# Two weight loads with a cast on the way, replaced by one load each and casts on ScalarE and GpSimd

## The chip, the cores and the metric

The kernel runs on one core of a Trainium2 chip. The metric is the device time of one launch in microseconds (us), the median over several runs. A core has five engines that run side by side and wait for each other through semaphores: TensorE (PE, matmuls, with its weight loads shown as PEld), VectorE (DVE), ScalarE (ACT), GpSimd (POOL) and SyncE (SP). Transfers between the device's memory and the core's on-chip memory are issued from a queue of SP or POOL and carried out by 16 DMA engines.

## What is computed

An attention with a few inducing points, followed by a feed-forward layer with a hard-swish. `x` is 4 batches of 12480 rows of 128 columns, `inducing` is 32 rows, the feed-forward layer is 2048 wide.

```python
def mab(q, kv):
    s = scale * (q @ kv.transpose(0, 2, 1))
    s = s - s.max(-1, keepdims=True)
    a = np.exp(s)
    a /= a.sum(-1, keepdims=True) + 1e-09
    return a @ kv
h = mab(I, x)                      # 32 x 128 for each batch
x2 = mab(x, h)                     # 12480 x 128 for each batch
u = x2 @ w_in                      # 128 -> 2048
g = u * np.clip(u + 3.0, 0.0, 6.0) / 6.0
out = g @ w_out                    # 2048 -> 128
```

## The kernel before

The kernel does not run the wide layer row by row. As long as the pre-activations stay small, hard-swish is a polynomial of second degree, and each row of the attention's output is a mixture of 32 rows of `h`; so the output of a row is a linear term plus a quadratic form in its 32 weights, and the coefficients of both can be made once for each batch. A check at the end (`bad_i`) leads to a direct path if that does not hold.

Each batch goes through three stages:

- **a**, the first attention: rows of x are cast to bf16 (`xb`), transposed on PE (`pt`, copied to `xT`), multiplied with the inducing points (`s`), exponentiated on ACT (`a`), and summed into `hnd` on PE; DVE sums the weights into `dacc`, the denominators.
- **c**, the coefficients: the column sums of the denominators on PE (`dps`, with a matrix of ones), their reciprocal (`rD`, DVE), the transposed `hnd` (`H` on ACT, `htp` on PE), their product `HT` (DVE), and from it `HTr` (ACT), `dH`, `W`, `Wd` (DVE). PE then multiplies `w_in_r` with `HTr` (`gp`, the linear part) and `w_in_b` with `dH` (`dpm`, the quadratic part); ACT and DVE square `dpm` into `sq`; PE multiplies `sq` with `w_out_b` (`cp`) and the activated `gp` with `w_out_r` (`lp`). The results are `BD` and `Cq`.
- **b**, the output: 25 chunks a batch, each with exponentials `TF` on ACT, products `TD` of them with a spread-out factor `d` on DVE, and matmuls `op` on PE with `BD` (line 795) and `Cq` (line 811), scaled into `os` by DVE and stored by SP. The factor `d` is spread over partitions by a DMA of SP (line 758), four chunks ahead.

The order on every engine is the order in which the program issues its instructions (`manual_schedule`); there is no planner. For batch 0, stage a runs alone (`a_first`), then stage c (`c_first`), then a loop of 100 chunks: chunk t of stage b with pieces of stages a and c of the next batch laid between by `fill`.

Loads of x are issued from POOL's queue, in this order before the loop: the seven loads of batch 0 (some in two parts), the four weight loads of `load_weights` (lines 158 to 163), the first two of batch 1. `w_in_b` and `w_out_b` are bf16 in on-chip memory, so their loads cast on the way; `w_in_r` and `w_out_r` keep 32 bits. The other four loads of batch 1 are held back: `load_held` (line 132) issues them when POOL has read a column of the fourth spread `d`, through the small copy `seen`. POOL is in order, so what stands before `seen` on POOL also stands before these loads. `xr` has five buffers; a load waits until its buffer has been read.

In `a_first`, the denominators end up in three pieces: `dacc` (folded by four adds on POOL, line 419), `dlast` (reduced on DVE, line 413 through 444) and the last piece (line 406 through 444). `c_den_part` adds one matmul with ones for each piece; a 32-bit matmul shows up as two passes on PE. `warm(n)` (line 174) issues n matmuls of zeros, 128x512, whose result nothing reads.

`c_first` opens like this:

```python
warm(1)
c_den(0)      # H on ACT, dps on PE, rD on DVE
warm(1)
c_HT(0)       # htp on PE, HT on DVE, HTr and HTb on ACT, dH W Wd on DVE
warm(1)
c_G(0, 0, 6)  # gp on PE
```

Of the kernel before, what the change touches and what calls it, by code (L numbers as in the profile page):

```python
# [9 lines left out]
FP32 = mybir.dt.float32  # L10
# [30 lines left out]
def kernel(  # L41
# [8 lines left out]
    nc = tc.nc  # L50
# [3 lines left out]
    F = moe_w_in.shape[1]  # L54
    FB = F // P
# [25 lines left out]
    with ExitStack() as es:  # L81
# [71 lines left out]
        w_in_b = const.tile([P, F], BF16, name="w_in_b")  # L153
        w_in_r = const.tile([P, F], FP32R, name="w_in_r")
        w_out_b = const.tile([P, FB, C], BF16, name="w_out_b")
        w_out_r = const.tile([P, FB, C], FP32R, name="w_out_r")

        def load_weights():
            w_out = moe_w_out.rearrange("(kb kp) c -> kp kb c", kp=P)
            nc.gpsimd.dma_start(w_in_b[:, :], moe_w_in[:, :])  # L160
            nc.gpsimd.dma_start(w_in_r[:, :], moe_w_in[:, :])
            nc.gpsimd.dma_start(w_out_b[:, :, :], w_out)
            nc.gpsimd.dma_start(w_out_r[:, :, :], w_out)


# [8 lines left out]
        def warm(n):  # L174

            wp = psF.tile([P, 512], FP32, name="wp", tag="fb")
            for _ in range(n):
                nc.tensor.matmul(wp[:, :], lhsT=wake[:, :P], rhs=wake[:, :])
# [57 lines left out]
        def side_bank(b, shape, dtype, name):  # L236

            if b == 0:
                turn[0] += 1
                if turn[0] % 2:  # L240
                    return psO.tile(shape, dtype, name=name, tag="op")
            return psF.tile(shape, dtype, name=name, tag="fb")
# [99 lines left out]
        def a_first():  # L342

            st = S[0]
            pieces = [(g, h, h + 8) for g in range(XBUF + 1) for h in (0, 8)]
            pieces.insert(2, (NF, 0, SL))
            last = len(pieces) - 1
            a1s = {}

            def cast(k):  # L350
                g, lo, hi = pieces[k]
                p = groups[g][1]
                if lo == 0:
                    xbs[(0, g)] = xbin.tile([P, TG, C], BF16, name="xb")
                xb, xf = xbs[(0, g)], xs[(0, g)]
                if hi - lo == 8 and (lo == 0 or k == last):
                    cuts = [(nc.scalar.copy, lo, lo + 4), (nc.vector.tensor_copy, lo + 4, hi)]
                else:
                    cuts = [(nc.scalar.copy, lo, hi)]
                for eng, i, j in cuts:  # L360
                    eng(xb[:p, i:j, :], xf[:p, i:j, :].bitcast(FP32))

            def transpose(k):
                g, lo, hi = pieces[k]
                t0, p, n = groups[g]
                step = 4 if k == last else 8
                for i in range(lo, hi, step):
                    j = min(i + step, hi)
                    pt = side_bank(0, [P, 1024], BF16, "pt")
                    for q in range(i, j):  # L370
                        nc.tensor.transpose(pt[:, (q - i) * p : (q - i + 1) * p], xbs[(0, g)][:p, q, :], ident_b[:p, :p])
                    eng = nc.scalar.copy if k == last and i > lo else nc.vector.tensor_copy
                    eng(st["xT"][:, t0 + i * p : t0 + j * p], pt[:, : (j - i) * p])

            def weights(k):
                g, lo, hi = pieces[k]
                t0, p, n = groups[g]
                s1 = side_bank(0, [P, 512], FP32, "s1")
                for q in range(lo, hi):
                    nc.tensor.matmul(  # L380
                        s1[:p, (q - lo) * M : (q - lo + 1) * M],
                        lhsT=st["xT"][:, t0 + q * p : t0 + (q + 1) * p],
                        rhs=I_T[:, :],
                    )
                w = (hi - lo) * M
                a1 = a1p.tile([P, TG * M], FP32R, name="a1")
                nc.scalar.activation(a1[:p, :w], s1[:p, :w], ACT.Exp, scale=scale)
                a1s[k] = a1

            def add(k):  # L390
                g, lo, hi = pieces[k]
                p, w, a1 = groups[g][1], (hi - lo) * M, a1s[k]
                for q in range(lo, hi):
                    nc.tensor.matmul(
                        st["hnd"][:M, :C],
                        lhsT=a1[:p, (q - lo) * M : (q - lo + 1) * M],
                        rhs=xs[(0, g)][:p, q, :],
                        start=(k == 0 and q == lo),
                        stop=(k == last and q == hi - 1),
                    )  # L400
                f = a1[:p, :w].bitcast(FP32)
                d = st["dacc"][:p, lo * M : hi * M]
                if g == 0:
                    nc.vector.tensor_copy(d, f)
                elif k == last:
                    c_red(0, f, p, hi - lo)
                elif k == last - 3:
                    st["dlast"] = cst.tile([P, 8 * M], FP32, name="dlast")
                    nc.vector.tensor_copy(st["dlast"][:, :], f)
                elif k > last - 3:  # L410
                    nc.vector.tensor_add(st["dlast"][:, :], st["dlast"][:, :], f)
                    if k == last - 1:
                        c_red(0, st["dlast"][:, :], P, 8)
                else:
                    nc.vector.tensor_add(d, d, f)
                if k == last - 4:
                    d = st["dacc"]
                    for h in (8, 4, 2, 1):
                        nc.gpsimd.tensor_add(d[:, : h * M], d[:, : h * M], d[:, h * M : 2 * h * M])
                    st.setdefault("dred", []).append(d[:, :M])  # L420
                if hi == groups[g][2]:
                    load_next(0, g)

            for k in range(3):
                cast(k)
            transpose(0)
            for k in range(last + 1):
                if k < last:
                    transpose(k + 1)
                weights(k)  # L430
                if k + 3 <= last:
                    cast(k + 3)
                if k:
                    add(k - 1)
                if k == 3:
                    half_rows()
            add(last)


        def c_red(b, src, p, n):  # L440
            st = S[b]
            st["reds"] = st.get("reds", -1) + 1
            dred = cst.tile([P, M], FP32, name=f"dred{st['reds']}")
            nc.vector.tensor_reduce(
                dred[:p, :], src.rearrange("p (s m) -> p m s", m=M), axis=AX.X, op=ALU.add
            )
            st.setdefault("dred", []).append(dred[:p, :])
# [182 lines left out]

        def c_first():

            warm(1)
            c_den(0)
            warm(1)
            c_HT(0)
            warm(1)
            c_G(0, 0, 6)
            sq = lambda *jbs: [c_sq(0, jb) for jb in jbs]
            cs = lambda *jcs: [c_C(0, jc) for jc in jcs]  # L640

            sg = lambda jb: (c_sq(0, jb), c_G(0, jb + 6, jb + 7))
            sg(0)
            sg(1)
            sg(2)
            b_pack(0, 0)
            b_e(0, 0)
            for c in range(4):
                b_spread(0, c)
            a_cast(1, 0, ((nc.gpsimd.tensor_copy, 0, 2), (nc.gpsimd.tensor_copy, 2, 4)))  # L650
            load_held(3)
            for jb in range(3, 7):
                sg(jb)
                cs(jb - 3)
            sg(7)
            b_f(0, 0)
            cs(4)
            sg(8)
            b_base(0, 0, 0)
            cs(5)  # L660
            sg(9)
            c_hs(0)
            b_base(0, 0, 1)
            cs(6)
            sq(10)
            cs(7)
            sq(11)
            b_r(0, 0)
            cs(8)
            sq(12)  # L670
            cs(9)
            sq(13)
            cs(10)
            b_base(0, 1, 0)
            sq(14)
            cs(11)
            sq(15)
            cs(12)
            c_L(0, 0)
            c_L(0, 1)  # L680
            b_base(0, 1, 1)
            c_BD(0)
            cs(13, 14, 15)
            b_prod(0, 0)
            c_tail(0)
            b_pack(0, 1)
            b_e(0, 1)
            c_max(0)
# [400 lines left out]
```

## Time and profile before

| what | us |
|---|---|
| median of 6 runs | 313.83 |
| lowest and highest | 313.18, 315.82 |
| the profiled execution | 313.89 |
| its span, first to last instruction | 312.1 |
| PE busy in the span | 298.3 |
| first matmul of `c_first` (a warm) | 24.87 |
| first `op` of the loop (line 795) | 39.74 |
| the same of batch 1 and of batch 2 | 114.46, 187.77 |
| granted TensorE clock, mean | 0.994 of full |

Times inside the profile count from the span's start. A line of the order of time has the start, the length, the engine, the line of the code, the operation, what it writes and reads, its shape and how many; in brackets the time that the engine was idle before it and what ended that. A line of the DMA issues ends with the size in KB and the median time from issue to landing. A line of the chain has the start, the length and what it was. The loads issued from POOL are the rows "POOLq".

### The profile page before, as it was taken

Reading aid. Unit: us, or ns where it says so; the run is one execution under the profiler, and the core shown is the slowest. Engines: PE = TensorE matmul, PEld = TensorE weight load, DVE = VectorE, ACT = ScalarE, POOL = GpSimd, SP = SyncE. Lnnn points to the kernel's source line nnn. Section 1 sums busy time; section 2 is a strip of 40 time slices with the busy share of each in tenths; the row PEclk is TensorE's granted clock in tenths of the full one; section 3 lists DMA queues with packets and bytes.
Section 4 is the critical chain, followed back from the end, with each engine's and each line's share of the span. In section 5 each row is a group of like instructions: output and inputs, shape, how many; then the busy total and the mean of one; then the engine's idle time right before and its main releaser. Section 6 shows DMA issues by size and latency. Waiting matters only on the chain.

```text
span 312.1 us, 9579 instructions
## 1 busy us (share of the span) xinstructions
PE 298.3 (96%) x3930; PEld 233.4 (75%) x3930; DVE 236.1 (76%) x539; ACT 226.3 (73%) x417; POOL 27.1 (9%) x64
## 2 busy tenths in 40 slices
PE   6899999999999999999999999999999999999991
PEld 2797777887677878888767878888767786777780
DVE  2697895978884868888695768788787577888883
ACT  3785869886589678886679759888668936777750
POOL 7631230100100000001000000000000000000000
PEclk9999999999999999999999999999999999999997
DMA  7999879988963444899966525555245424666643
GB/s 218 414 340 285 312 237 396 308 312 264 335 229 130 109 165 83 276 321 318 321 201 188 177 97 137 205 155 185 86 137 189 159 50 170 202 215 213 221 168 155
DMA packets 26769, 67.73 MB, mean 217 GB/s; under 512 B 5184, under 2 KB 19552, under 8 KB 20832
## 3 DMA queue, kind: packets, MB, share of 16 engines
q1 hardware_dynamic: 18160, 38.36, 37.7%
q0 software_dynamic: 8560, 28.71, 29.9%
q8 instruction: 32, 0.52, 0.7%
q14 instruction: 17, 0.14, 0.1%
HBM read 29.77 MB, written 25.56 MB: 177 GB/s over the span
## 4 chain that ended last, share of the span: by engine, by line
PE 73%; DMA 10%; DVE 6%; ACT 4%; issue 2%; POOL 2%; SPq 0%; DVEq 0%; ACTq 0%; POOLq 0%
PE op L811 27%; PE bp L771 11%; PE op L795 7%; DMA xr<-in_x_dram 6%; PE hnd L292 6%; PE pt L270 4%; DMA d<-dk 4%; PE cp L592 4%; ACT sq L583 2%; PE s L278 2%; PE pp L742 2%; PE dpm L572 2%; PE ep L698 2%; PE sp L712 1%; DVE os L827 1%
## 5 line engine op out<-in xcount | busy, mean ns | idle before, releaser
L778 ACT ACTIVATE TF<-bp 128x512 bf16<-128x512 f32 (+1 forms) x200 | 116.7, 596 | 38.2 <-PE rp L731 21.0
L811 PE MATMUL op<-Cq,TF 128*128 128x128 bf16 (+1 forms) x800 | 109.3, 223 | 0.0
L811 PE MATMUL op<-Cq,TD 128*128 128x128 bf16 (+1 forms) x800 | 105.9, 219 | 0.0
L827 DVE TENSOR_TENSOR os<-op,r_all 128x512 f32<-128x512 f32 (+1 forms) x100 | 68.4, 684 | 18.6 <-PE op L811 17.8
L771 PE MATMUL bp<-xT,W 128*128 128x512 bf16 (+1 forms) x200 | 75.2, 376 | 0.6 <-ACT TF L778 0.5
L811 PEld LDWEIGHTS <-TF 128*128 128x128 bf16 (+1 forms) x800 | 50.5, 98 | 33.7 <-issue 24.7
L787 DVE TENSOR_TENSOR TD<-TF,d 128x1024 bf16<-128x1024 bf16 (+1 forms) x100 | 66.9, 669 | 5.2 <-ACT TF L778 3.4
L811 PEld LDWEIGHTS <-TD 128*128 128x128 bf16 (+1 forms) x800 | 61.3, 98 | 1.0 <-DVE TD L787 0.2
L795 PE MATMUL op<-BD,nf 128*128 128x512 f32 (+1 forms) x100 | 53.3, 533 | 0.5 <-DVE os L827 0.4
L583 ACT ACTIVATE sq<-dpm 128x512 bf16<-128x512 f32 x60 | 34.8, 629 | 5.5 <-PE dpm L572 3.1
L261 ACT CAST xb<-xr 128x1024 bf16<-128x1024 f32 x34 | 35.6, 1055 | 2.8 <-DMA xr<-in_x_dram 2.8
L732 DVE RECIPROCAL r_all<-rp 128x4 f32<-128x4 f32 (+1 forms) x100 | 17.8, 178 | 23.3 <-PE rp L731 22.9
L731 PE MATMUL rp<-one,nf 128*128 128x4 f32 (+1 forms) x100 | 34.5, 345 | 0.3
L271 DVE COPY xT<-pt 128x1024 bf16<-128x1024 bf16 (+1 forms) x42 | 25.8, 618 | 6.3 <-PE pt L270 5.8
L122 POOL DMA_DIRECT2D xr<-in_x_dram x25 | 13.6, 550 | 146.1 <-PE rp L731 44.9
L749 ACT ACTIVATE dk<-pp 128x512 bf16<-128x512 f32 (+1 forms) x28 | 15.7, 560 | 11.6 <-PE pp L742 10.2
L292 PE MATMUL hnd<-xr,a 128*32 128x128 f32 x288 | 24.1, 226 | 0.0
L572 PE MATMUL dpm<-dH,w_in_b 128*128 128x512 bf16 x64 | 23.3, 380 | 0.1
L270 PE MATMUL pt<-ident_b,xb 128*128 128x128 bf16 x300 | 23.3, 218 | 0.0
L771 PEld LDWEIGHTS <-W 128*128 128x128 bf16 x200 | 19.5, 97 | 5.0 <-issue 3.4
L592 PE MATMUL cp<-w_out_b,sq 128*128 128x128 bf16 x256 | 22.7, 220 | 0.0
L514 PE MATMUL gp<-HTr,w_in_r 128*128 128x32 f32 x64 | 21.3, 358 | 0.3 <-ACT HTr L492 0.3
(129 smaller groups left out, 391.4 us busy)
## 6 DMA issues: line engine op xcount, KB each, us to landing
out_dram<-os SPq DMA_DIRECT2D x24, 1024.0 KB, 4.1
xr<-in_x_dram POOLq DMA_DIRECT2D x21, 1024.0 KB, 7.5
d<-dk SPq DMA_DIRECT2D x96, 128.0 KB, 4.2
xr<-in_x_dram POOLq DMA_DIRECT2D x4, 512.0 KB, 8.2
x<-in_x_dram POOLq DMA_DIRECT2D x2, 512.0 KB, 13.9
w_in_r<-in_moe_w_in_dram POOLq DMA_DIRECT2D x1, 1024.0 KB, 15.7
w_out_r<-in_moe_w_out_dram POOLq DMA_DIRECT2D x1, 1024.0 KB, 17.5
w_in_b<-in_moe_w_in_dram POOLq DMA_DIRECT2D x1, 512.0 KB, 13.4
```

Source lines behind the costliest of these rows:

```text
L261: eng(xb[:p, lo:hi, :], xs[(b, g)][:p, lo:hi, :].bitcast(FP32))
L270: nc.tensor.transpose(pt[:, (i - lo) * p : (i - lo + 1) * p], xb[:p, i, :], ident_b[:p, :p])
L292: nc.tensor.matmul(st["hnd"][:M, :C], lhsT=a1[:p, i * M : (i + 1) * M], rhs=xs[(b, g)][:p, i, :], start=(g == 0 and i == 0), stop=(g == NG ...
L583: nc.scalar.activation(sq[:, :], dpm[:, :], ACT.Square)
L592: nc.tensor.matmul(st["cp"][:, k * C : (k + 1) * C], lhsT=sq[:, k * P : (k + 1) * P], rhs=w_out_b[:, jc, :], start=(jc == 0 and k == 0), s ...
L731: nc.tensor.matmul(rp[:p, :SL], lhsT=nf[:, j * p : (j + 1) * p], rhs=one4[:, :])
L771: nc.tensor.matmul(bp[:, :w], lhsT=st["W"][:, k].rearrange("p m i -> p (m i)"), rhs=st["xT"][:, c0 : c0 + w],)
L778: nc.scalar.activation(st[("x", c)][:, k, :w], bp[:, :w], ACT.Exp, scale=scale)
L787: nc.vector.tensor_mul(u[:, :, :w], t[:, :, :w], d[:, :w].unsqueeze(1).to_broadcast([P, 2, w]))
L795: nc.tensor.matmul(op[:p, :], lhsT=st[("nf", g)][:, j * p : (j + 1) * p], rhs=st["BD"][:, :], start=True, stop=False, skip_group_check=True,)
L811: nc.tensor.matmul(op[:p, s * C : (s + 1) * C], lhsT=T[k][:, s * p : (s + 1) * p], rhs=st["Cq"][:, k, :], start=False, stop=(s == SL - 1 a ...
L827: nc.vector.tensor_mul(ot[:p, j * SL : (j + 1) * SL, :], op[:p, :].rearrange("p (s c) -> p s c", c=C), r_all[:p, b, c, :].unsqueeze(2).to_ ...
```

## The change

It has four parts, all in the first batch.

1. `load_weights` loads only `w_in_r` and `w_out_r`; the two loads that cast to bf16 are gone.
2. `c_first` makes `w_in_b` from `w_in_r` with two copies on ACT, one ahead of `c_den(0)` (so ahead of `H`) and one behind it (ahead of `HTr`). It makes `w_out_b` from `w_out_r` with two copies on POOL, behind the folding adds and ahead of the casts of batch 1's first piece and of `seen`.
3. The folded `dacc` is added to the reduced `dlast` on DVE, between the two reduces, so that two pieces instead of three go into `dps`.
4. The first two `warm(1)` of `c_first` become `warm(2)`.

```diff
         def load_weights():
             w_out = moe_w_out.rearrange("(kb kp) c -> kp kb c", kp=P)
-            nc.gpsimd.dma_start(w_in_b[:, :], moe_w_in[:, :])
             nc.gpsimd.dma_start(w_in_r[:, :], moe_w_in[:, :])
-            nc.gpsimd.dma_start(w_out_b[:, :, :], w_out)
             nc.gpsimd.dma_start(w_out_r[:, :, :], w_out)
...
                     if k == last - 1:
                         c_red(0, st["dlast"][:, :], P, 8)
+                        d1, d2 = st["dred"]
+                        nc.vector.tensor_add(d2, d2, d1)
+                        st["dred"] = [d2]
...
         def c_first():
 
-            warm(1)
+            warm(2)
+            nc.scalar.copy(w_in_b[:, : F // 2], w_in_r[:, : F // 2].bitcast(FP32))
             c_den(0)
-            warm(1)
+            nc.scalar.copy(w_in_b[:, F // 2 :], w_in_r[:, F // 2 :].bitcast(FP32))
+            for h in (0, FB // 2):
+                hs = slice(h, h + FB // 2)
+                nc.gpsimd.tensor_copy(w_out_b[:, hs, :], w_out_r[:, hs, :].bitcast(FP32))
+            warm(2)
             c_HT(0)
             warm(1)
             c_G(0, 0, 6)
```

## The prediction

> **What bounds the kernel now.** I read the page first: busy shares, then the DMA issues, then the chain of waits, and only then the order of time from 5 to 60 us, because the diff touches nothing that runs later than 40 us except through what it makes late or early.
>
> ```profile
> span 312.1 us, 9579 instructions
> PE 298.3 (96%) x3930; PEld 233.4 (75%) x3930; DVE 236.1 (76%) x539; ACT 226.3 (73%) x417; POOL 27.1 (9%) x64
> ```
>
> TensorE (PE) is busy 96% of the span. From 40 us on it is the bound, so an edit is worth what it adds to or takes from PE's stalls, no more. Next, the DMA issues (KB each, us from issue to landing) and, from the order of time, the four weight issues on POOL:
>
> ```profile
> w_in_r<-in_moe_w_in_dram POOLq DMA_DIRECT2D x1, 1024.0 KB, 15.7
> w_out_r<-in_moe_w_out_dram POOLq DMA_DIRECT2D x1, 1024.0 KB, 17.5
> w_in_b<-in_moe_w_in_dram POOLq DMA_DIRECT2D x1, 512.0 KB, 13.4
> w_out_b<-in_moe_w_out_dram POOLq DMA_DIRECT2D x1, 512.0 KB, 16.5
> ```
> ```profile
> 10.26 0.55 POOL L160 DMA_DIRECT2D w_in_b<-in_moe_w_in_dram  x1
> 10.80 0.54 POOL L161 DMA_DIRECT2D w_in_r<-in_moe_w_in_dram  x1
> 12.79 1.17 POOL L162 DMA_DIRECT2D w_out_b<-in_moe_w_out_dram  x1 [1.45 <-DMA xr<-in_x_dram]
> 15.29 1.15 POOL L163 DMA_DIRECT2D w_out_r<-in_moe_w_out_dram  x1 [1.33 <-DVE xT L373]
> ```
>
> Issue plus time to landing gives when each arrives. The last piece of x for batch 0, by the view of tile x, was issued at 7.47 and took 13.9: 21.4. Then w_in_b 23.7, w_in_r 26.5, w_out_b 29.3, w_out_r 32.8. The view of tile xr has 19.1 as its longest, which is the load issued at 19.42: 38.5. The xr load issued at 16.85 lies between, by 35.7 (POOL starts its cast of it at 35.76). The steps are 2.3, 2.8, 2.8, 3.5, 2.9, 2.8 us: the queue works as a line, one load behind another, and a load that writes 512 KB costs nearly as much of it as one that writes 1024 KB.
>
> What hangs on that line is in the chain of waits (start, us, what), and then in the order of time:
>
> ```profile
> 31.93 7.56 DMA d<-dk
> 39.54 0.28 POOL seen L135
> 40.32 7.00 DMA xr<-in_x_dram
> ```
> ```profile
> 47.40 1.05 ACT L261 CAST xb<-xr 128x1024 bf16<-128x1024 f32 x1 [2.75 <-DMA xr<-in_x_dram]
> 49.00 0.38 PE L771 MATMUL bp<-xT,W 128*128 128x512 bf16 x1 [0.55 <-ACT TF L778]
> ```
>
> The fourth spread d waits 7.56 us behind the line; `seen` waits for d; the held loads of batch 1 wait for `seen`; the first big one takes 7.00 us and lands at 47.32; ACT has been idle for 2.75 us; TF, behind that cast on ACT, is late; PE stops. It is the one DMA wait of ACT in 40 to 60 us.
>
> **What the change removes.** Two loads, 2.3 + 2.8 = 5.1 us of the line. Nothing of x moves, since x stands ahead of the weights. w_in_r takes w_in_b's place: 21.4 + 2.8 = 24.2. w_out_r: 24.2 + 3.5 = 27.7. The two xr loads: 30.6 and 33.4. POOL also issues w_out_r and the two xr loads earlier (w_out_b waited 1.45 us for an xr load to land before it could go out, and the issues after it followed); a load still lands no earlier than its place in the line.
>
> Then d: the fourth spread is issued at 31.93 + 0.4 (the front's delay, below). It lands about 1 us after the line empties in the old run (39.5 against 38.5), which would be 34.4, but a spread on a quiet queue takes 2.5 us in the trace (the ones of 2.5 to 2.6 us near 117 to 122 us), so 34.8. `seen` follows, unless POOL is still casting: its last cast of batch 1's first piece ends at 30.6 + 2 x 1.04 = 32.7. The held load goes out at 40.32 - 4.7 = 35.6 and lands, at the same 7.0, at 42.6. ACT came to this cast at 47.40 - 2.75 = 44.65 and will at 45.0: the wait is gone with 2.4 us to spare, and the two loads behind it, 2.9 us each, arrive before their casts at 49.32 and 52.65 too.
>
> Worth on PE: from the op matmul at 48.17 to the bp at 49.00 passed 0.83, where the same pair at 45.61 and 45.73 took 0.12: 0.71. The pair of op at 49.44 and 49.73 took 0.29, at 43.23 and 43.35 0.12: 0.17. The 16 s matmuls at 49.85 took 0.84 (they wait for an xT copy that DVE had behind the late TD), those at 43.46 0.56: 0.28. Sum 1.16 us. Bounds: 0.55 (the wait the row itself names) and 1.41 (first op<-BD of a batch to the next batch's first: 39.74 to 114.46 is 74.72, 114.46 to 187.77 is 73.31). I take 1.16; after the stall ACT has to catch up, and without it nothing is late next that the trace shows.
>
> **What it adds ahead of the loop.** These are the rows between the last matmul of the first stage and the first of the second:
>
> ```profile
> 24.36 0.61 DVE L444 TENSOR_REDUCE dred<-dlast 128x32 f32<-128x256 f32 x1
> 24.89 0.58 DVE L444 TENSOR_REDUCE dred<-a 128x32 f32<-128x256 f32 x1
> 25.07 0.26 ACT L472 COPY H<-hnd 32x128 f32<-32x128 f32 x1 [0.75 <-PE hnd L394]
> 25.77 0.38 PE L178 MATMUL wp<-wake 128*128 128x512 bf16 x1
> 25.97 0.36 DVE L477 RECIPROCAL rD<-dps 128x32 f32<-128x32 f32 x1 [0.50 <-PE dps L460]
> 26.08 0.24 PE L483 MATMUL htp<-ident,H 32*128 32x32 f32 x1
> 26.44 0.23 DVE L486 TENSOR_TENSOR HT<-htp,rD 128x64 f32<-128x64 f32 x1
> 26.70 0.22 ACT L492 CAST HTr<-HT 128x32 fp32r<-128x32 f32 x1 [1.37 <-DVE HT L486]
> ```
>
> *The DVE add.* It needs the first reduce (ends 24.97) and POOL's last add (24.06 + 0.39 = 24.45, covered). No row shows a 128x32 add f32 alone; the nearest, L504 on 128x32 at 28.16, takes 0.20, with the next DVE instruction 0.10 behind it. So the second reduce starts at 24.97 + 0.04 + 0.10 = 25.11 instead of 24.89, +0.22, and with it dps and rD: 26.19.
>
> *Matmuls.* Six dps passes become four, which saves two steps of 0.11, but PE waits for the second reduce at that point: worth nothing. The first extra warm takes their place. The second, between dps and htp, is on the path: the warm at 24.87 holds PE until the first dps at 25.10, 0.23, and the chain puts 0.22 to a matmul of 512 columns. htp starts at 26.08 + 0.22 + 0.22 = 26.52, ends 26.76; HT at 26.84 instead of 26.44. Everything behind, HTr, gp, dH, dpm, moves by that: +0.40. Bounds: 0.22 (htp hidden behind rD) and 0.55 (eight warms in a row at 3.34 take 2.60 us, so (2.60 - 0.38) / 7 = 0.32 each, and 0.22 of the add).
>
> *ACT casts.* Each is 128x1024 f32 to bf16: 1.05 us by the L361 and L261 rows. The last Exp of the stage ends at 23.93 + 0.39 = 24.32 and w_in_r is there at 24.2. First half to 25.4, H (0.26) to 25.65, second half to 26.7, HTr wanted at 27.1. H is wanted by htp at 26.52. Both casts lie in ACT's idle time: 0. The cover is 0.4 us: if w_in_r lands after 24.6, the second half holds HTr, and each us of lateness is a us at the end.
>
> *POOL casts.* 1.04 each by the L261 POOL row. w_out_r at 27.7, halves done at 28.8 and 29.8; the first cp, which needs the first half, is at 29.56 + 0.40 = 29.96, the ninth some 4 us later. Behind them on POOL: the xr casts (wanted by PE at 40.9) and `seen`, both covered above. Cost 0, with a cover of 1.2 us.
>
> *POOL beside DVE.* These casts run while DVE makes dH and W from two SBUF operands. The rows for such a meeting: L411 adds, 0.42 us beside POOL's adds at 22.25 to 24.45, and L415 adds of the same shape 0.42 with POOL idle; but the L409 copy takes 0.44 beside POOL where the same copy at L404 takes 0.28 alone. So 0 to 2 x 1.04 = 2.08 if each cast shut DVE out entirely. I take 0, by the row of the same kind.
>
> [...]
>
> **Sum.** -1.16 + 0.40 = -0.76. The profiled execution took 313.89 (span 312.1 and 1.8 around it), 0.06 above the median 313.83 of the six. 313.89 - 0.76 = 313.13, less 0.06: 313.1.
>
> **Rivals.** *The stall is replaced* (0.15). PE waits as long for DVE or another tile in the first loop, and only the front's cost is left: 313.8 + 0.4 = 314.2. For it: DVE and ACT are at 2.00 of 2 us in several stretches there; against it: batch 1, with the same work, runs 1.41 shorter.
>
> *More is relieved* (0.17). All 1.41 comes back, the front is hidden, and PE's stop of about 0.5 us at 40.3 to 40.6 (op waiting for Cq) goes as well: 313.8 - 1.9 = 311.9. Against it: Cq waits for DVE work on cp, not for a load.
>
> *The line is not a line* (0.10), the slower one. If landings are paced by something other than the bytes ahead, w_in_r lands at 26.5 as now. ACT is in order, so H waits: 26.5 + 1.05 + 0.26 = 27.8, then htp, HT at 28.2, the second half until 28.9, HTr, gp at 29.1 instead of 26.96: +2.15, and no load is earlier, so nothing comes back: 313.8 + 2.15 = 316.0. Against it are six even steps of the line. Were the stall's gain kept, it would decide from a landing of 24.6 + 0.76 = 25.4 on.
>
> *POOL shuts DVE out* (0.08): 313.1 + 2.08 = 315.2.
>
> **How the numbers follow.** The forecast has 0.50, with 312.6 to 313.8 as its own range (stall 0.55 to 1.41, front 0.22 to 0.55). The range reaches down to the second rival and up to the last, 311.8 to 315.2, leaving out the third and tails. 0.5%, or 1.57 us, is about what a measurement of this kernel can tell from no change. Faster by more: the second rival, 0.17. Slower by more: the third and half of the last, 0.14. Within: 0.69.
>
> **What would show it.** Right: w_in_r lands near 24.2 and w_out_r near 27.7; HT starts 0.3 to 0.5 later; `seen` near 35; no DMA wait of ACT before the L261 cast near 45; a first batch within 0.5 us of 73.3. Wrong: an ACT cast of w_in ended by a DMA wait past 24.6; dH or W rows of 1 us or more; PE idle before cp; a stop of bp on TF that stays.

## The result, and the profile after

| | before | changed |
|---|---|---|
| median, us (runs) | 314.02 (71) | 317.44 (34) |
| ratio, changed to before | | 1.0077, 95% interval 1.0057 to 1.0098 |
| profiled execution, us | 313.89 | 318.12 |
| its span, us | 312.1 | 316.3 |
| mean granted TensorE clock in it | 0.994 | 0.986 |

The changed kernel is slower by 0.8%. The medians are of all runs; the ratio leaves out the slow ones, over 1.5% above the fastest of the same kernel, so it is not the quotient of the two medians. The forecast was 313.1 us and its range ended at 315.2.

The top of the page of the changed kernel shows where to look. In the line PEclk each digit is a fortieth of the span, 7.9 us, and 9 stands for 90% or more of full clock:

```profile
span 316.3 us, 9580 instructions
PE 302.0 (95%) x3930; PEld 235.2 (74%) x3930; DVE 239.0 (76%) x540; ACT 228.9 (72%) x419; POOL 27.8 (9%) x64
PEclk9999699999999999999999999999999999999998
L259 ACT CAST xb<-xr 128x1024 bf16<-128x1024 f32 x34 | 35.5, 1052 | 0.0
w_in_r<-in_moe_w_in_dram POOLq DMA_DIRECT2D x1, 1024.0 KB, 13.8
w_out_r<-in_moe_w_out_dram POOLq DMA_DIRECT2D x1, 1024.0 KB, 16.8
```

Three things stand there. The same 3930 matmuls kept PE busy for 302.0 us instead of 298.3, and the fifth slice, 31.6 to 39.5 us, has a reduced clock that the page of before has nowhere but in its last slice. The group of ACT casts on L259 has no idle time ahead of it; in the kernel before the same group (L261) had these 2.8 us:

```profile
L261 ACT CAST xb<-xr 128x1024 bf16<-128x1024 f32 x34 | 35.6, 1055 | 2.8 <-DMA xr<-in_x_dram 2.8
```

And the loads come early: issued at 10.28 and 10.82, w_in_r lands at 24.08 and w_out_r at 27.64; 24.2 and 27.7 had been worked out. So what was to be relieved was relieved. From the first `op` matmul of the loop to the first of batch 1 it is 45.29 to 118.86, 73.57 us, where the kernel before took 74.72 (how much of that the earlier loads are worth is taken up at e8). The loss lies ahead of that: the first `op` starts 5.55 us later than before, at 45.29 instead of 39.74.

In order of time (start, us, engine, line, operation), the front of the changed kernel:

```profile
27.00 0.22 DVE L487 TENSOR_TENSOR HT<-htp,rD 128x64 f32<-128x64 f32 x1 [0.25 <-PE htp L484]
27.25 0.58 DVE L499 TENSOR_TENSOR dH<-HT 128x256 bf16<-128x256 f32 x1
27.70 2.38 POOL L640 CAST w_out_b<-w_out_r 128x1024 bf16<-128x1024 f32 x2 [3.16 <-DMA w_out_r<-in_moe_w_out_dram]
27.75 1.42 DVE L500 TENSOR_TENSOR dH<-HT 128x256 bf16<-128x256 f32 x1
29.09 1.42 DVE L502 TENSOR_TENSOR W<-HT 128x256 bf16<-128x256 f32 x1
29.22 0.39 PE L573 MATMUL dpm<-dH,w_in_b 128*128 128x512 bf16 x1 [0.85 <-DVE dH L500]
30.27 2.13 POOL L259 CAST xb<-xr 128x1024 bf16<-128x1024 f32 x2 [0.19 <-ACT sq L584]
30.43 1.03 DVE L505 TENSOR_TENSOR Wd<-HT 128x32 bf16<-128x32 f32 x1
31.51 0.62 PE L748 MATMUL pp<-xT,Wd 128*32 128x512 bf16 x4 [1.37 <-DVE Wd L505]
33.37 0.63 PE L573 MATMUL dpm<-dH,w_in_b 128*128 128x512 bf16 x1
```

and the same DVE instructions of the kernel before, where POOL did nothing at that time:

```profile
26.70 0.58 DVE L498 TENSOR_TENSOR dH<-HT 128x256 bf16<-128x256 f32 x1
27.18 0.58 DVE L499 TENSOR_TENSOR dH<-HT 128x256 bf16<-128x256 f32 x1
27.68 0.58 DVE L501 TENSOR_TENSOR W<-HT 128x256 bf16<-128x256 f32 x1
28.16 0.20 DVE L504 TENSOR_TENSOR Wd<-HT 128x32 bf16<-128x32 f32 x1
```

The first `dH` takes 0.58 in both. From the moment POOL starts to cast, the other `dH` and `W` take 1.42 each and `Wd` 1.03 instead of 0.20. PE waits for them twice, 0.85 and 1.37 us, as the brackets say. And from then on the `dpm` matmul that took 0.39 at 29.22 takes 0.63 at 33.37: the clock. The view of stretches of the changed kernel gives it (stretch, length, busy us and instructions of PE, PEld, DVE, ACT, POOL, then granted clock, DMA share, GB/s):

```profile
28.00:30.77 2.77, 1.29 (x10) 0.89 (x9) 2.77 (x3) 1.11 (x2) 2.58 (x3) 1.00 0.91 349
30.77:37.60 6.83, 6.09 (x39) 4.21 (x40) 3.54 (x7) 3.37 (x6) 1.63 (x2) 0.50 0.37 87
```

PE was busy for 1.29 of the 2.77 us up to 30.77; then it had half its clock for 6.83 us.

Five distances in the order of time split the loss. They are used for every kernel below:

| us | before | changed | difference |
|---|---|---|---|
| start of `HT` | 26.44 | 27.00 | +0.56 |
| `HT` to first `dpm` | 1.48 | 2.23 | +0.75 |
| first `dpm` to first `pp` | 0.84 | 2.29 | +1.45 |
| first `pp` to first `op` | 10.99 | 13.77 | +2.78 |
| first `op` to batch 1's first `op` | 74.72 | 73.57 | -1.15 |

The rest of the span differs by -0.17; together that is +4.22. The two spans, 316.3 and 312.1, differ by 4.2.

### The profile page after: what moved, and what is told of

It is laid out like the page before. It is cut to its first block, busy times and chain, and to the rows that moved or that the text cites. A ratio compares the mean times of both kernels' runs of the same rounds, so it can differ in the third digit from the quotient of the medians.

```text
span 316.3 us, 9580 instructions
## 1 busy us (share of the span) xinstructions
PE 302.0 (95%) x3930; PEld 235.2 (74%) x3930; DVE 239.0 (76%) x540; ACT 228.9 (72%) x419; POOL 27.8 (9%) x64
## 4 chain that ended last, share of the span: by engine, by line
PE 78%; DVE 9%; DMA 7%; issue 2%; POOL 1%; ACT 1%; DVEq 0%; ACTq 0%; POOLq 0%
PE op L817 28%; PE bp L777 12%; PE op L801 7%; PE hnd L290 6%; PE cp L593 5%; PE pt L268 5%; DMA x<-in_x_dram 4%; PE dpm L573 3%; PE pp L748 3%; PE s L276 3%; DMA d<-dk 2%; PE ep L704 2%; PE sp L718 2%; DVE os L833 1%; DVE dred L445 1%
## 5 line engine op out<-in xcount | busy, mean ns | idle before, releaser
L259 ACT CAST xb<-xr 128x1024 bf16<-128x1024 f32 x34 | 35.5, 1052 | 0.0
L573 PE MATMUL dpm<-dH,w_in_b 128*128 128x512 bf16 x64 | 24.6, 400 | 0.9 <-DVE dH L500 0.9
L593 PE MATMUL cp<-w_out_b,sq 128*128 128x128 bf16 x256 | 23.8, 227 | 0.0
L515 PE MATMUL gp<-HTr,w_in_r 128*128 128x32 f32 x64 | 22.4, 375 | 0.2 <-ACT HTr L493 0.2
```

The costliest lines, as they stand in the source:

```text
L259: eng(xb[:p, lo:hi, :], xs[(b, g)][:p, lo:hi, :].bitcast(FP32))
L593: nc.tensor.matmul(st["cp"][:, k * C : (k + 1) * C], lhsT=sq[:, k * P : (k + 1) * P], rhs=w_out_b[:, jc, :], start=(jc == 0 and k == 0), s ...
```

## The experiments

The first theory: POOL's casts and DVE's instructions with two inputs in SBUF hold each other up (SBUF is the on-chip memory of the tiles; PSUM, where PE writes its results, is another), and the pauses that this makes on PE bring the half clock with them. Rivals: the front (the folded sums and the second warms) is what delays things; the clock falls for a reason of its own; POOL's writes, not its reads, disturb DVE.

In the table, "half clock" is the stretch up to the first `op` in which the view of stretches shows 0.50.

| kernel | `HT` | to `dpm` | to `pp` | to `op` | first `op` | batch 0 | half clock |
|---|---|---|---|---|---|---|---|
| before | 26.44 | 1.48 | 0.84 | 10.99 | 39.74 | 74.72 | none |
| changed | 27.00 | 2.23 | 2.29 | 13.77 | 45.29 | 73.57 | 30.77 to 37.60 |
| e1_wout_dma | 26.92 | 1.39 | 0.85 | 10.98 | 40.14 | 73.58 | none |
| e2_pool_late | 26.90 | 1.38 | 0.85 | 10.98 | 40.11 | 77.95 | none |
| e3_warm_cover | 27.90 | 3.02 | 2.61 | 10.97 | 44.50 | 73.57 | 10.75 to 14.16 |
| e4_before_pool_reads | 26.49 | 2.22 | 1.35 | 12.54 | 42.60 | 73.58 | 30.14 to 33.55 |
| e5_before_pool_writes | 27.21 | 1.49 | 0.84 | 10.98 | 40.52 | 74.73 | 10.74 to 14.16 |
| after_again | 27.22 | 2.23 | 2.29 | 12.92 | 44.66 | 73.59 | 29.19 to 36.02 |
| after_third | 26.95 | 2.23 | 2.29 | 13.46 | 44.93 | 75.87 | 30.05 to 36.88 |
| e6_pool_late_old_front | 26.46 | 1.39 | 0.85 | 10.98 | 39.68 | 76.10 | none |
| e6_again | 26.48 | 1.38 | 0.85 | 10.98 | 39.69 | 76.24 | none |
| e7_win_only | 26.51 | 1.40 | 0.85 | 10.97 | 39.74 | 73.58 | none |
| e7_again | 26.47 | 1.39 | 0.85 | 10.98 | 39.68 | 73.58 | none |
| e8_sums_warms_only | 27.64 | 1.47 | 0.84 | 10.98 | 40.93 | 73.56 | 10.79 to 14.20 |

### e1_wout_dma: w_out_b by DMA again, no POOL casts of weights

```diff
             nc.gpsimd.dma_start(w_in_r[:, :], moe_w_in[:, :])
+            nc.gpsimd.dma_start(w_out_b[:, :, :], w_out)
             nc.gpsimd.dma_start(w_out_r[:, :, :], w_out)
...
-            for h in (0, FB // 2):
-                hs = slice(h, h + FB // 2)
-                nc.gpsimd.tensor_copy(w_out_b[:, hs, :], w_out_r[:, hs, :].bitcast(FP32))
```

> The changed kernel with w_out_b loaded by the casting DMA again and without the two GpSimd casts; the ScalarE casts of w_in, the folded sums and the four warms stay. Theory (the GpSimd casts read on-chip memory while VectorE makes dH, W and Wd from two operands in it, and one shuts the other out; PE waits, and its clock then falls to half): the dH and W rows are 0.58 us again instead of 1.42, Wd 0.20 instead of 1.03, dpm starts near 28.4, the first op of the loop near 40.3 instead of 45.29, no stretch of half clock before the end, time 313.2 to 313.9. Rival (the ScalarE casts, the VectorE add or the warms delay the front): the first op stays near 45 and the time at 316 to 318. Loads: w_in_r lands near 24.1, w_out_b 26.9, w_out_r 30.4, the two xr 33.2 and 36.1.

Measured: 314.55 us, ratio 0.9997 (0.9957 to 1.0038); the profiled execution took 313.64, within the expected 313.2 to 313.9, the median lies above it. With POOL silent there, DVE has its old lengths although the folded sums, both second warms and the ACT casts are still in:

```profile
27.67 0.58 DVE L501 TENSOR_TENSOR dH<-HT 128x256 bf16<-128x256 f32 x1
28.16 0.58 DVE L503 TENSOR_TENSOR W<-HT 128x256 bf16<-128x256 f32 x1
28.31 0.39 PE L574 MATMUL dpm<-dH,w_in_b 128*128 128x512 bf16 x1
28.66 0.19 DVE L506 TENSOR_TENSOR Wd<-HT 128x32 bf16<-128x32 f32 x1
```

The first `op` starts at 40.14, 5.15 us ahead of the changed kernel's. The front as a main cause falls: it is all here, and costs 0.40 at the first `op`. Of the 5.55 us, the rest goes with the POOL casts. The first batch has its gain here too, 73.58 (e8 says more of that).

### e2_pool_late: the POOL casts behind DVE's work

```diff
-            for h in (0, FB // 2):
-                hs = slice(h, h + FB // 2)
-                nc.gpsimd.tensor_copy(w_out_b[:, hs, :], w_out_r[:, hs, :].bitcast(FP32))
             warm(2)
             c_HT(0)
+            gate = cst.tile([P, 1], BF16, name="gate")
+            nc.gpsimd.tensor_copy(gate[:, :], S[0]["Wd"][:, 0:1])
+            for h in range(0, FB, FB // 4):
+                hs = slice(h, h + FB // 4)
+                nc.gpsimd.tensor_copy(w_out_b[:, hs, :], w_out_r[:, hs, :].bitcast(FP32))
```

> The changed kernel with the GpSimd casts of w_out behind a one-column GpSimd copy that reads Wd, so that they start when VectorE is done with dH, W and Wd, and in four quarters instead of two halves. Theory (collision): dH and W rows 0.58, Wd 0.20; the casts run beside VectorE work that has one operand in PSUM, which is not slowed; first quarter ready near 29.6, where the first cp wants it at about 30; first op near 40.3, ScalarE does not wait for xr near 45, time 313.0 to 313.5. Rival (GpSimd slows any VectorE instruction, whatever it reads): the rows of d, sq and nf near 29 to 32 us become longer than 0.69 and the time stays over 315. Rival (front): as in the run with w_out_b from the DMA, 316 to 318.

Measured: 315.98 us, ratio 1.0013 (0.9964 to 1.0063). In the order of time of this kernel POOL waits 4.45 us for `Wd`, and `W` is back to 0.57:

```profile
28.14 0.57 DVE L502 TENSOR_TENSOR W<-HT 128x256 bf16<-128x256 f32 x1
28.88 0.19 POOL L641 COPY gate<-Wd 128x1 bf16<-128x1 bf16 x1 [4.45 <-DVE Wd L505]
29.00 2.29 POOL L644 CAST w_out_b<-w_out_r 128x512 bf16<-128x512 f32 x4
```

The same casts, a little later, cost the front nothing: first `op` at 40.11, no half clock before it. That is what the theory said of the front. The rival that GpSimd slows any DVE instruction falls as well: `d` at 28.97 and `sq` at 29.69, which have an input in PSUM, run beside the casts and take 0.69 each, as `d` and `sq` do in the kernel before. What the theory said of the time, 313.0 to 313.5, came in two of the ten executions (312.99 and 313.02) and not in the median. The profile shows one reason, at another place: in the first batch `TD` waits for a spread `d` from 84.2 to 87.3 us, PE stops, and the clock halves once more. The row of waits between 80 and 92 us (who, for what: us in total, times, longest), then the stretch:

```profile
DVE TD L795 <- DMA d<-dk: 3.1, 1, 3.1
```
```profile
87.53:94.36 6.83, 6.06 (x35) 4.45 (x35) 5.82 (x16) 2.77 (x7) 0.00 (x0) 0.50 0.41 163
```

The batch takes 77.95 instead of 73.58. More of this at e6.

### e3_warm_cover: matmuls of zeros where PE waits

```diff
             sg = lambda jb: (c_sq(0, jb), c_G(0, jb + 6, jb + 7))
+            warm(5)
             sg(0)
...
             sg(2)
+            warm(8)
             b_pack(0, 0)
```

> The changed kernel with five more warm matmuls before the first dpm and eight more before the first pp, the two places where PE stands idle for VectorE. Theory (the clock falls because PE stands idle there): dH and W rows stay at 1.42, but there is no stretch of half clock before the end, in any run; first op near 42.5, time 314.4 to 314.8, which is where the fastest runs of the changed kernel lie, with a mean clock near 0.994 in every run. Rival (the clock falls for another reason, as the power of the denser work): half clock near 31 to 38 stays and runs spread up to 318.

Measured: 317.1 us, ratio 1.0071 (1.0034 to 1.0109). The time expected was missed by over 2 us, yet the run tells the clock and the collision apart. In its view of stretches the clock stays whole where the changed kernel lost it, and is half at a much earlier place:

```profile
10.75:14.16 3.41, 3.41 (x35) 2.97 (x33) 2.07 (x6) 2.68 (x5) 1.84 (x4) 0.50 1.09 423
30.80:37.60 6.80, 6.68 (x62) 4.41 (x62) 5.82 (x10) 4.54 (x9) 2.32 (x2) 1.00 0.25 60
```

From `pp` to `op` it is 10.97 us, as before. So the 2.78 us of that distance are the clock, and what brings it is PE's idleness there: with 13 matmuls that compute nothing in the gaps it stayed away, in this one profile (whose steps of the clock also lie elsewhere; see the last section). Expensive were the other terms. The early half clock put `HT` at 27.90; w_out_r was there in time, so POOL's casts now met all three large DVE instructions (1.38, 1.41, 1.42) and `Wd` (1.03), and `HT` to `pp` took 5.63 instead of 4.52. The collision alone, with a whole clock behind it, costs 3.3 us here.

### e4_before_pool_reads and e5_before_pool_writes: the collision put into the kernel before

Both add work on POOL to the kernel before, whose result nothing reads; all loads, sums and warms are as they were.

```diff
             c_den(0)
+            dummy = cst.tile([P, 512], BF16, name="dummy")
+            nc.gpsimd.tensor_copy(dummy[:, 0:1], w_in_r[:, 0:1].bitcast(FP32))
+            for h in range(0, F, 512):
+                nc.gpsimd.tensor_copy(dummy[:, :], w_in_r[:, h : h + 512].bitcast(FP32))
             warm(1)
```

and in e5, in place of that loop:

```diff
+            for h in range(8):
+                nc.gpsimd.memset(dummy[:, :], 0.0)
```

> The kernel before with four more GpSimd casts, 128x512 f32 to bf16 each, from w_in_r into a tile that nothing reads, in the place where the change has its casts; they start when w_in_r lands, near 26.6. Theory (a GpSimd instruction that reads on-chip memory shuts out a VectorE instruction with two operands there): dH and W rows rise from 0.58 to 1.0 or more each, while VectorE rows with an operand in PSUM (d<-dpm, 0.69) do not. Rival (the landing of the loads, or the ScalarE casts, slow VectorE): dH and W stay at 0.58.

> The same, but with eight GpSimd memsets of the same tile in place of the casts (after a one-column copy from w_in_r that makes them start when it lands). They write and read nothing. Theory (it is GpSimd's reading that collides with the second operand): dH and W rows stay at 0.58. Rival (any GpSimd work collides): they rise as with the casts.

e4, one run: 315.62 us, with 313.75 for the kernel before on the same chip. e5: 314.67 against the same 313.75. In order of time, e4:

```profile
26.61 3.36 POOL L638 CAST dummy<-w_in_r 128x512 bf16<-128x512 f32 x4
26.75 0.91 DVE L498 TENSOR_TENSOR dH<-HT 128x256 bf16<-128x256 f32 x1
27.57 1.00 DVE L499 TENSOR_TENSOR dH<-HT 128x256 bf16<-128x256 f32 x1
28.49 0.99 DVE L501 TENSOR_TENSOR W<-HT 128x256 bf16<-128x256 f32 x1
29.40 0.60 DVE L504 TENSOR_TENSOR Wd<-HT 128x32 bf16<-128x32 f32 x1
```

and e5:

```profile
26.59 4.61 POOL L638 MEMSET dummy<- 128x512 bf16 x8
27.47 0.58 DVE L498 TENSOR_TENSOR dH<-HT 128x256 bf16<-128x256 f32 x1
27.97 0.58 DVE L499 TENSOR_TENSOR dH<-HT 128x256 bf16<-128x256 f32 x1
28.47 0.56 DVE L501 TENSOR_TENSOR W<-HT 128x256 bf16<-128x256 f32 x1
28.96 0.18 DVE L504 TENSOR_TENSOR Wd<-HT 128x32 bf16<-128x32 f32 x1
```

POOL is busy under all four DVE instructions in both. Where it only writes, DVE keeps its lengths (0.56 to 0.58, 0.18). Where it reads, they grow, and so do POOL's: four casts of 128x512 take 3.36 us against 2.29 in e2, where DVE had nothing of the kind beside them. The growth goes with the length of POOL's instruction: +0.33 to +0.42 beside casts of 128x512 (0.61 to 0.63 each in e2), +0.84 beside casts of 128x1024 (1.04 alone). What the two runs show is that a DVE instruction with two SBUF inputs is drawn out beside a GpSimd one that reads SBUF (`dH` and `W` 0.91 to 1.00 in e4), not beside one that only writes (0.56 to 0.58 in e5). One row does not fit: the adds into `dlast` of stage a (L411 in the kernel before), with both inputs in SBUF, take 0.41 to 0.43 us in every profile beside POOL's short adds, which read SBUF too. Why these are not drawn out is not shown.

e4 also shows the second half of the theory in a kernel with nothing of the change in it: delays of 0.74 and 0.51 us (1.48 to 2.22, 0.84 to 1.35) are followed by half a clock from 30.14 to 33.55, and `pp` to `op` takes 12.54. e5 kept the whole clock there. Its own loss is not the memsets' doing: DVE's last adds of stage a were 0.77 us late before the memsets ran, and the half clock ahead of them, 10.74 to 14.16, came to e3 and e8 as well. Its first batch, 74.73, is as long as in the profile of before, but by another wait, for a spread `d`:

```profile
65.09 0.69 DVE L791 TENSOR_TENSOR TD<-TF,d 128x1024 bf16<-128x1024 bf16 x1 [3.22 <-DMA d<-dk]
```

### after_again and after_third: the changed kernel, profiled twice more

> The changed kernel itself, profiled a second time. [...] If the first op of the loop starts before 42.5, there is no half clock between 25 and 40 us, and the span is 312.5 to 313.

> The changed kernel profiled a third time. By the two profiles so far: HT to dpm 2.2 us and dpm to pp 2.3 us in every profile (1.5 and 0.8 in the kernel before), whatever the clock does; pp to the first op of the loop 11.0 where the clock stays up, 12.9 to 13.8 where it falls to half.

Measured: 317.65 and 320.04 us. `HT` to `dpm` and `dpm` to `pp` are 2.23 and 2.29 in all three profiles of the changed kernel. The half clock lasts 6.83 us in each, but starts at 30.77, 29.19 and 30.05, and so catches a different amount of PE's work: `pp` to `op` 13.77, 12.92, 13.46. The start lies a whole number of steps of 3.41 us behind the first rise of the clock: 23.89 us, 7 steps, in all three (rises at 6.88, 5.30 and 6.16). after_third shows, in its order of time, the two halves of POOL's casts apart and so how the engines take turns:

```profile
27.55 1.15 POOL L640 CAST w_out_b<-w_out_r 128x1024 bf16<-128x1024 f32 x1 [3.07 <-DMA w_out_r<-in_moe_w_out_dram]
27.70 1.42 DVE L500 TENSOR_TENSOR dH<-HT 128x256 bf16<-128x256 f32 x1
28.64 1.39 POOL L640 CAST w_out_b<-w_out_r 128x1024 bf16<-128x1024 f32 x1
29.04 1.42 DVE L502 TENSOR_TENSOR W<-HT 128x256 bf16<-128x256 f32 x1
30.15 1.22 POOL L259 CAST xb<-xr 128x1024 bf16<-128x1024 f32 x1
30.38 1.03 DVE L505 TENSOR_TENSOR Wd<-HT 128x32 bf16<-128x32 f32 x1
```

A cast ends at 28.70, the `dH` beside it 0.42 later; the next cast, 1.39 long instead of 1.04, ends at 30.03, `W` 0.43 later; the cast of x ends at 31.37, the small `Wd` at 31.41. These ends fit an order in which each DVE instruction waits out the cast beside it and the next cast waits for it. Note the third of them: it is no weight but batch 1's x, which before was cast from 35.76 us on and now, its load being early, comes down on `Wd`. The gain on the DMA queue sharpened the collision.

after_third has in addition the late spread of e2: `TD` waits 2.7 us for `d` near 92 us, and batch 0 takes 75.87. Its expectation named the three distances of the front, and they came.

### e6_pool_late_old_front and e6_again: e2 with the sums and warms of before

```diff
-                        d1, d2 = st["dred"]
-                        nc.vector.tensor_add(d2, d2, d1)
-                        st["dred"] = [d2]
...
-            warm(2)
+            warm(1)
...
-            warm(2)
+            warm(1)
```

> As the run with the late GpSimd casts in quarters, but with the sums unfolded and one warm in each place, as before the change. Theory: the whole front is as before, HT near 26.44, first op near 39.8; the late load of xr is gone, so the first batch takes 73.6 instead of 74.7; time 313.9 - 1.16 = 312.7, under the kernel before. If the folded sums and warms are no cost but a gain (PE kept warm), it is slower than the run with them, over 313.5.

> The kernel with late GpSimd casts in quarters and the old front, profiled a second time. First profile: VectorE waited 2.2 us for a spread d at 84 to 86 us, PE stood still for 1.7 us and its clock fell to half for 3.41 us. If that wait is a matter of the run, it is gone here, the first batch takes 73.6 us and the span is near 310.8; if the earlier loads make it, it is here again near the same place.

e6: 315.29 us, ratio 1.0009 (0.9963 to 1.0055), where 312.7 was expected. The front is as worked out (`HT` at 26.46, first `op` at 39.68, 0.43 ahead of e2). The first batch again is not: 76.10, and 76.24 in the repeat (315.13 us). In order of time, e6_again:

```profile
86.79 0.69 DVE L792 TENSOR_TENSOR TD<-TF,d 128x1024 bf16<-128x1024 bf16 x1 [3.05 <-DMA d<-dk]
```

The spread of that chunk is issued at 76.33 and lands at 86.70; in e7, below, it lands at 83.31. The wait is in e2, e6, e6_again and after_third, 2.2 to 3.1 us between 84 and 92 us, and their first batches are 2.3 to 4.4 us longer than 73.58. At this place it is in no profile of a kernel that loads w_out_b by DMA (before, e1, e4, e5, both e7, e8), and absent from three of the seven of kernels that do not (two of the changed kernel, and e3). But waits of the same kind stand at other places: 3.2 us at 65 us in e5, with all four loads of before, and 2.0 us near 154 us in after_again. So a late spread needs none of the change's edits. What decides it was not settled.

### e8_sums_warms_only: the kernel before, with folded sums and second warms

```diff
                         c_red(0, st["dlast"][:, :], P, 8)
+                        d1, d2 = st["dred"]
+                        nc.vector.tensor_add(d2, d2, d1)
+                        st["dred"] = [d2]
...
-            warm(1)
+            warm(2)
             c_den(0)
-            warm(1)
+            warm(2)
```

> The kernel before with only the folded sums and the two more warms; loads as before. It measures the front term alone: predicted HT at 26.84 instead of 26.44, first op at 40.1; the runs with the change's front have HT at 26.9 to 27.0. Time 314.2 to 314.4.

Measured: 314.48 us, one run. Its profile has the early half clock, so it is compared with e5, which has the same one at the same place: `HT` 27.64 against 27.21, +0.43; first `op` 40.93 against 40.52, +0.41. Folding the sums and doubling the warms costs 0.4 us and brings nothing. The first batch took 73.56 with all four weight loads in place, as in e4 (73.58). The 2.75 us wait of ACT that the kernel before shows near 45 us is absent from both, for two reasons. The front is later, so ACT comes to its cast later: at 45.84 in e8 and 47.40 in e4, where before it came at 44.65. And the first held load took 5.43 us in e8 and 5.06 in e4, not the 7.00 of the profile of before. At 5.4 us and with the front of before a wait of about 1.1 us would be left (an estimate: 40.32 + 5.4 - 44.65).

### e7_win_only and e7_again: only w_in cast on ACT

The kernel before, with one of the four parts of the change: w_in_b by the two casts on ACT. w_out_b is loaded, the sums and warms are untouched.

```diff
-            nc.gpsimd.dma_start(w_in_b[:, :], moe_w_in[:, :])
             nc.gpsimd.dma_start(w_in_r[:, :], moe_w_in[:, :])
...
             warm(1)
+            nc.scalar.copy(w_in_b[:, : F // 2], w_in_r[:, : F // 2].bitcast(FP32))
             c_den(0)
+            nc.scalar.copy(w_in_b[:, F // 2 :], w_in_r[:, F // 2 :].bitcast(FP32))
             warm(1)
```

> The kernel before with only the load of w_in_b replaced, by the two ScalarE casts; w_out_b is loaded with a cast as before, sums and warms as before. Theory: no GpSimd cast, so no collision; ScalarE's casts are hidden, the front is as before (HT 26.44, first op 39.74); the loads are 2.3 us earlier, enough for the wait of 2.75 us near 45 to shrink to 0.5 or less; time 312.8 to 313.4, ratio 0.996 to 0.999. Rival (ScalarE's casts delay H or HTr): HT later than 26.8 and the time above 313.8.

> The kernel with only the load of w_in_b replaced, timed again in five rounds, since its first interval reached from 0.992 to 1.001. If its gain is the wait of ScalarE near 45 us that is gone, the ratio is again 0.996 to 0.998 and the first batch takes 73.6 us in the profile.

Measured: 312.71 us, ratio 0.9967 (0.9924 to 1.0009), and 313.67 us, ratio 0.9952 (0.9907 to 0.9996); both spans 310.8. In order of time, e7_win_only:

```profile
24.27 1.04 ACT L633 CAST w_in_b<-w_in_r 128x1024 bf16<-128x1024 f32 x1
25.36 1.04 ACT L635 CAST w_in_b<-w_in_r 128x1024 bf16<-128x1024 f32 x1
26.51 0.23 DVE L485 TENSOR_TENSOR HT<-htp,rD 128x64 f32<-128x64 f32 x1
39.74 0.58 PE L796 MATMUL op<-BD,nf 128*128 128x512 f32 x1
113.32 0.58 PE L796 MATMUL op<-BD,nf 128*128 128x512 f32 x1
```

Both casts lie in ACT's idle time and `HT` is where it was within 0.07 us. The first `op` starts at 39.74, the very time of the kernel before, and the first batch takes 73.58: the first held load goes out at 37.73 instead of 40.32 and lands at 43.28, ahead of ACT, which comes to it at 44.55. Both medians lie below the lowest time of the changed kernel, 314.37. Against the kernel before, the gain is 0.3 to 0.5%: one interval just includes no change, the other ends at 0.9996.

## Why the prediction was wrong

**What failed** is the step "POOL beside DVE": "So 0 to 2 x 1.04 = 2.08 if each cast shut DVE out entirely. I take 0, by the row of the same kind." The sign of being wrong that the prediction named, `dH` or `W` rows of 1 us or more, is there (1.42). It is the other end that holds: +0.75 and +1.45, 2.20 in all, a little above the upper bound, since it left out the cast of x, whose loads the change itself brings forward onto `Wd`. The rows chosen, the L411 adds, were near by the kind of DVE instruction but not by POOL's: beside them POOL did short adds of 0.38 to 0.46 us, not casts of 1.04. That this is why they kept their length is not shown; by the growth beside e4's casts some 0.2 us could have been expected of such adds too (an estimate: 0.33 / 0.62 x 0.39). The row that pointed the other way, the L409 copy at 0.44 against 0.28, was named and set aside. The runs went with that row: 1.42 for 0.58 and 1.03 for 0.20 beside casts that read SBUF, no growth beside e5's writes.

**What was missing** is a term: what a pause of PE does to the clock. The last rival, "POOL shuts DVE out", had the mechanism with a chance of 0.08, but priced it at the pauses alone, 315.2. The half clock adds 2.78 to the distance from `pp` to `op`; e3 shows it by taking the clock's fall away (10.97), e4 by bringing it about without the change (12.54). With both terms the prediction's own sum, 313.13 for the profiled execution, comes out: 313.13 + 2.20 + 2.78 = 318.11, and +0.16 for the rest of `HT`'s delay and -0.17 for the rest of the span leave 318.10. The profile took 318.12.

**What was right.** *The line of loads*: 24.2 and 27.7 for the weights against 24.08 and 27.64; 30.6 and 33.4 for x against 30.12 and 32.58. *The stall's worth*: 1.16 against 1.15, in part by luck. The 7.00 us of the first held load, from which the wait of 2.75 comes, are of the one execution of before: the same load took 5.06 to 5.46 us in e4, e5 and e8, whose loads are the same. And in the changed kernel the late front alone brings ACT to its cast 5.5 us later. So this term is probably worth less in the median than in the profile; e7, with the front of before, gained 0.3 to 0.5%. *The ACT casts*: no cost, as e7 shows by itself. *The front*: 0.40 worked out; +0.47 in the profile of the changed kernel (`HT` 0.56 later, of which 0.09 lay ahead of the first warm), 0.43 in e8 against e5. (Its upper bound, 0.55, was priced too high: of the eight warms at 3.34 the first four started 0.40 to 0.43 us apart, ahead of the clock's first rise at 4.79, the last four 0.21 to 0.22.) `seen` was put near 35 and came at 38.04, because the front was late; it did no harm, as the held loads were still in time.

**The other rivals.** *The stall is replaced*: not in the profile of the changed kernel, 73.57; the late spreads in e2, e5, e6 and after_third are such cases, at other places. *More is relieved*: no; and PE's stop at 40.3, put at about 0.5 us there, was nearer 0.2 (the two `op` at 40.30 took 0.47, the next such pairs 0.27). *The line is not a line*: it is one.

**What stays open.** Over the 36 executions of the changed kernel that are listed with a clock, the time goes with the mean granted clock: eight with 0.993 to 0.995 took 314.4 to 314.8, six with 0.988 to 0.990 315.7 to 317.7, the other 22, at 0.986 or less, 316.5 to 321.7. So there are executions in which the clock hardly fell and only 0.4 to 0.8 us over the median before was left. No profile is of such a one, and how large the collision was in them isn't known. What makes the spread late in e2, e5, e6 and after_third is open too.

## What to carry to other kernels

Before work is laid on GpSimd because it is idle, look at what DVE does at that moment: if DVE has instructions with two inputs in SBUF there and the GpSimd work reads SBUF, count for each up to the length of the other's instruction (an estimate from the +0.84 here beside a cast of 1.04 us, and +0.33 to +0.42 beside casts of 0.61 to 0.63), and place the GpSimd work after them, as e2 did (its front lost nothing, though its median gained nothing either), or leave that part to the load, as e1 and e7 did. When a bound comes from "the nearest row", the row has to be near in both of the instructions that meet. And a pause ahead of a stretch that PE bounds can cost more than its own length: here PE's waits of 0.85 and 1.37 us were followed by half a clock, which added 2.78 us.

## What the runs showed of the hardware that was not expected

- The clock fell after pauses much shorter than the 3.41 us of its stretches: 0.85 and 1.37 us of idle PE with some work between (PE busy 1.29 of 2.77 us) were followed by half a clock for 6.83 us, the 0.74 and 0.51 us that e4 adds by 3.41 us. Ahead of the end of each kernel, all stretches at half clock are 3.41 us or twice that. They start at other times from one execution to the next (30.77, 29.19, 30.05), but always a whole number of 3.41 us steps behind the clock's first rise: one step in e3, e5 and e8, seven in the changed kernel and e4, 24 in e2 and e6 (81.92 us).
- How long a pause is does not decide alone. In e6 PE stood still for 1.55 us inside one such step (busy 1.87 of 3.41 us), and the clock fell; in e6_again it stood still for 2.38 us across the border of two (busy 2.06 and 2.22), and the clock stayed whole. What does decide was not shown.
- The clock is also half from 10.75 to 14.16 us in some profiles (e3, e5, e8) and not in others, and puts `HT` 0.8 to 1.0 us later. In these three the clock first rises at 7.33 to 7.38 us, in the other eleven between 4.79 and 7.21.
